# Retention, then two mixtures of experts, on one core: logits two tile steps behind the rows, and the first expert's low weight parts made on VectorE

## The chip, the cores and the metric

One core of one Trainium2 chip runs the whole program in one launch. The metric is the time of one execution in microseconds (us); lower is better. Instructions are issued in order on each of five engines: TensorE (PE, matrix products), VectorE (DVE), ScalarE (ACT), GpSimd (POOL) and SyncE (SP, which here issues most of the transfers).

## The reference

Three layers, each fed by the one before. Only what is computed is kept here.

```python
# 1: batch 8, heads 8, seq 576, head_dim 64
scores = scale * q @ k.T
Dmat   = where(rel >= 0, gamma[h] ** rel, 0.0)       # decay by distance, causal
x      = (scores * Dmat) @ v                         # then laid out as 4608 rows of 512
# 2: 8 experts, each w1 512x1024 and w2 1024x512
logits = x @ w_gate                                  # the row's best expert, by argmax
out    = gate_w * (relu(x @ w1[e]) @ w2[e])
# 3: the same shapes; rows are assigned to experts greedily by their logits,
#    with a capacity of 576 rows for each expert
```

## The kernel before

The 4608 rows are 36 tiles of 128 (lines 141 to 153). Nine tiles make a pair of batches: tiles 0 and 1 of the nine begin the two sequences, and tile 8 holds the last 64 rows of both (`tail`). `attention` (line 128) walks over steps s; in a step each stage function of the table at line 318 is called for tile s - offset, in the order of the table. Every instruction issued there is pinned to that order on its engine (`Pinned`, `InOrder`, lines 107 to 125), and the trace gives all of them the line L114. So a wait on one instruction holds up all that stands behind it on the same engine.

The stages, with the offset of the kernel before:

- `load` (-6): SP loads k, q and v of a tile. `pre` (-2): POOL scales v into `vf`. `kturn`, `qturn` (-2): PE transposes k and q, ACT copies them to `kT` and `qT`.
- `begun` (0): PE multiplies q with the running state, `pO<-qT,st` (nothing for the first tile of a sequence). `scores` (0): PE makes `pS<-qT,kT` and the update of the state (`tp<-vf,k`, not for a tail); DVE masks the scores into `s` in two halves and adds up the state `st`.
- `outputs` (0): PE makes `pO<-s,vf`, eight products with the first half of `s` and eight with the second; DVE scales the result into the tile's rows, `xT`.
- `split` (1): ACT rounds `xT` to a 16-bit high part `xTh`; POOL subtracts, giving the low part `xTl`. Two buffers each.
- `logits` (1): PE multiplies the four blocks of `xTh` and the four of `xTl` with the gate's weights `wg1s`; ACT copies the result into `lgs`.
- `rows` (1): PE transposes `xT`, ACT copies it as `xr`. Three or four tiles make a group, fewer at the end; for a group, `best` (1), `first` (2) and `gates` (3) choose the experts on DVE and ACT, and `store` sends the rows to `Xs` in memory one step after `gates`.

On PE a step thus runs: `begun`, `scores`, the transposes of k, the logits, the output products, the transposes of the rows, the transposes of q.

Two generators run beside the steps, one `next` at the end of a step (lines 328 to 330). `load_half` (line 372) loads the first weights of expert 0 in four pieces (`stage`), from step 4 on, and in steps 13, 16, 19 and 22 it casts a piece to 16 bits on ACT (`w1h`) and makes the low part `w1l` of it. Its argument `dve` says how many pieces' low parts DVE makes; the others take two POOL instructions, a product in place (`stage<-stage`) and a difference. `early` (line 685), from step 30 on, builds lists of rows for expert 0 out of the first 27 tiles, gathers three blocks of 128 rows with POOL's transfers, and two, three and four steps later normalises one block each: a square sum and a scaled copy on ACT, a handful of small operations and a difference on DVE, then a transposing transfer into `xT` of expert 0.

After attention comes `moe1`: expert 0's first products (`ph<-xT,w1h`, line 532) begin with those three blocks. Everything from there on is placed by lists of steps and a scheduler that the change does not touch.

Of the kernel before, what the change touches and what calls it, by code (L numbers as in the profile page):

```python
# [10 lines left out]
F16 = mybir.dt.float16  # L11
# [6 lines left out]
NT = 36  # L18
# [5 lines left out]
SA = 3  # L24
LEAD_IN = 6
CAST = (4, 3)
EARLY = (30, 1)
T0 = (76, 88)
LATE = 3
SOON = 3  # L30
# [97 lines left out]
def attention(k, q, kk_, v, wg1, consts, X, after):  # L128
# [6 lines left out]
    wk = ctx.enter_context(tc.tile_pool(name="wk", bufs=3))  # L135
# [4 lines left out]
    NT = 36  # L140
# [104 lines left out]
        nc.vector.tensor_tensor(pairs(d.xT), d.o, pairs(G[:, d.j]), op=OP.mult)  # L245

    def split(d):
        d.xh = wk.tile([128, 4, 128], F16, name="xTh", bufs=2)
        d.xl = wk.tile([128, 4, 128], F16, name="xTl", bufs=2)
        nc.scalar.activation(d.xh, d.xT, AF.Copy)  # L250
        nc.gpsimd.tensor_tensor(d.xl, d.xT, d.xh, op=OP.subtract)

# [60 lines left out]
    def store():  # L313
        while pend:
            p = pend.pop(0)
            nc.sync.dma_start(Xv[:, p.t0:p.t0 + p.n, :], p.xrows[:, :p.n, :])

    stages = [(load, -LEAD_IN), (split, 1), (pre, -2), (begun, 0), (scores, 0), (kturn, -2), (logits, 1), (outputs, 0), (rows, 1),
              (qturn, -2), (gates, 3), (first, 2), (best, 1)]
    for s in range(-LEAD_IN, NT + 4):  # L320
        store()
        if s == 2 - LEAD_IN:
            nc.sync.dma_start(G[:, 0], consts[:, NC:NC + 512].rearrange("p (h q) -> p h q", q=128))
            k.wg1 = split_gate(k, wg1, "wg1", True)
        for f, off in stages:
            if 0 <= s - off < NT:
                f(D[s - off])
        for g, at0, step in after:
            if s >= at0 and (s - at0) % step == 0:
                next(g, None)  # L330
# [41 lines left out]
def load_half(k, o, w, n, dve=0, spare=False, steps=True, behind=False, spread=False):  # L372


    tc, nc = k.tc, k.nc
    if n == 1:
        o.wp = k.wp2 if k.wn % 2 else k.wp
        k.wn += 1
        o.w1h = o.wp.tile([128, 4, 1024], F16, name="w1h")
        o.w1l = o.wp.tile([128, 4, 1024], F16, name="w1l")  # L380
        h, l, shape, v = o.w1h, o.w1l, [128, 4, 256], w.rearrange("(c p) f -> p c f", p=128)
        at = lambda x, i: x[:, :, i * 256:(i + 1) * 256]
    else:
        if spare:
            o.w2h, o.w2l = (k.wp2.tile([128, 4, 1024], F16, name=x).rearrange("p c (a f) -> p (c a) f", a=2) for x in ("w1h", "w1l"))
        else:
            o.w2h = o.wp.tile([128, 8, 512], F16, name="w2h")
            o.w2l = o.wp.tile([128, 8, 512], F16, name="w2l")
        h, l, shape, v = o.w2h, o.w2l, [128, 2, 512], w.rearrange("(c p) f -> p c f", p=128)
        at = lambda x, i: x[:, 2 * i:2 * i + 2, :]  # L390

    def load(i):
        t = k.wp.tile(shape, F32, name="stage", bufs=3)
        d = nc.sync.dma_start(t, at(v, i))
        if behind:
            tc.keep_in_program_order(d)
        stages.append(t)

    stages = []
    for i in range(3):  # L400
        load(i)
        if spread and i < 2:
            yield
    for i in range(4):
        yield
        t = stages[i]
        if i >= dve:
            if steps:
                pe(k, nc.scalar.activation(at(h, i), t, AF.Copy, scale=128.0))
            else:  # L410
                nc.scalar.activation(at(h, i), t, AF.Copy, scale=128.0)
            pe(k, nc.gpsimd.tensor_scalar(t, t, 128.0, 1.0, op0=OP.mult, op1=OP.mult))
            nc.gpsimd.tensor_tensor(at(l, i), t, at(h, i), op=OP.subtract)
        else:
            d = nc.scalar.activation(at(h, i), t, AF.Copy, scale=128.0)  # L415
            if steps:
                pe(k, d)
            d = nc.vector.scalar_tensor_tensor(at(l, i), t, 128.0, at(h, i), op0=OP.mult, op1=OP.subtract)  # L418
            if steps:
                pe(k, d)  # L420
        if i == (1 if spread else 0):
            load(3)
    if n == 2:
        o.whole = True
# [260 lines left out]
def early(k, X):  # L685


    nc = k.nc
    k.nA = k.cp.tile([128, 4], F32, name="nA")
    OA = k.OH[:, 0, 0:TA]  # L690
    inc = k.lp.tile([128, TA], F16, name="incA", bufs=1)
    nc.vector.tensor_tensor_scan(inc, k.one_h[:, 0:TA], OA, 0.0, op0=OP.mult, op1=OP.add)
    pb = k.tp([128, 2])
    nc.tensor.matmul(pb[:, 0:1], k.lt_h, inc[:, TA - 1:TA], start=True, stop=True)
    nc.tensor.matmul(pb[:, 1:2], k.one_h, inc[:, TA - 1:TA], start=True, stop=True)
    nc.vector.tensor_copy(k.nA[:, 0:2], pb)
    nc.vector.tensor_tensor(k.nA[:, 2:3], k.nA[:, 0:1], inc[:, TA - 1:TA], op=OP.add)
    nc.vector.tensor_scalar(k.nA[:, 3:4], k.nA[:, 0:1], -1.0, 128.0 * SA, op0=OP.mult, op1=OP.add)
    V = k.lp.tile([128, 1, TA + 4], F16, name="VA", bufs=1)
    tables(k, V, TA, inc[:, None, :], k.nA[:, 0:1])  # L700
    nc.vector.scalar_tensor_tensor(OA, inc, k.nA[:, 3:4], OA, op0=OP.is_gt, op1=OP.mult)
    ix, _ = lists(k, V[:, 0, :], TA, k.nA[:, 0:1], k.nA[:, 2:3], SA, k.slot)

    g = k.wp.tile([128, 8, 512], F16, name="w2h").rearrange("p f d -> p (f d)").bitcast(F32)
    h = k.wp.tile([128, 8, 512], F16, name="w2l").rearrange("p f d -> p (f d)")
    sc = k.cp.tile([128, SA, 6], F32, name="scA")
    rows = [gather(k, X[0:128 * TA, :], ix[:, s:s + 1], xg=g[:, W * s:W * (s + 1)]) for s in range(SA)]
    k.early = new_xT(k), []
    yield
    for s in range(SA):  # L710
        yield
        x, c = normalise(k, rows[s], to=(h[:, 1024 * s:1024 * (s + 1)], sc[:, s, :]))
        turn(k, x, k.early[0], s)
        k.early[1].append(c)
# [910 lines left out]
def program(tc, q, kk, v, wg1, w11, w12, wg2, w21, w22, consts, out, dbg=None):  # L1625
    nc = tc.nc
    ctx = ExitStack()
    k = K()
    k.pin = False
    setup(k, tc, nc, ctx, consts)  # L1630
    moe_setup(k, ctx)
    X = tc.dram_tile([128 * NT, W], F32, name="Xs")
    X1 = tc.dram_tile([128 * NS, W], F32, name="X1s")
    LG = tc.dram_tile([128 * NS, 8], F32, name="LGsd")
    k.wgl = split_gate(k, wg2, "wg2")
    select_setup(k)
    k.w = {0: K()}
    attention(k, q, kk, v, wg1, consts, X, [(load_half(k, k.w[0], w11[0], 1, spread=True), *CAST), (early(k, X), *EARLY)])
    open_ffn(k)
    rest = moe1(k, X, X1, w11, w12)  # L1640
    k.pin = False
    overflow(k, X, X1, LG, w11, w12)
    k.wn, k.xn, k.yn = 8, 9, 0
    k.pin = True
    moe2(k, X1, w21, w22, out, rest)
    k.pin = False
    anew(k, X1, w21, w22, out)
    if dbg:
        dbg(k, X, X1, LG)
    k.fctx.close()  # L1650
    ctx.close()
# [25 lines left out]
```

## Time and profile before

| | |
|---|---|
| time, median of 3 runs | 1142.6 us (1140.8 to 1146.78) |
| the profiled execution | 1146.84 us, of which the span from first to last instruction is 1145.0 |
| mean granted TensorE clock in it | 0.965 of full speed |
| PE busy | 1056.3 us, 92% |
| DVE, ACT, POOL busy | 608.1, 436.7, 309.5 us |
| 0 to 200 us: PE busy in each 50 us | 40.91, 46.00, 40.82, 43.67 |
| 200 to 250 us | 40.13, at a mean clock of 0.80 |
| 300 to 400 us: PE busy in each 50 us | 50.00, 50.00 |

Times inside the profile count from the span's start. A line of the timeline gives the start, the duration, the engine, the line and the operation, what is written <- what is read, the shape and how many instructions are merged into it; in brackets how long the engine sat idle before it and what ended that. A granted clock of 1.00 is 2.4 GHz, of 0.50 is 1.2 GHz.

### The profile page before, as it was taken

The page shows a single profiled execution, that of the slowest core. Times are in us where ns is not written, and L with a number is a line of the kernel's source. Part 1 is how long each engine was busy: PE and PEld are TensorE (multiplying, and loading weights), DVE is VectorE, ACT ScalarE, POOL GpSimd, SP SyncE. Part 2 cuts the span into 40 slices and gives each one's busy share as a digit, 9 for nine tenths or more (in the row PEclk, how much of TensorE's full clock was granted, in tenths as well). Part 3 has the DMA queues.
Part 4 walks back from the last instruction along what each step waited for, and adds up shares of the span by engine and source line. Part 5 has one row for each costly group of instructions (what it writes and reads, how often), then busy time and mean ns, then how long its engine had stood idle before and what let it go on. Part 6 is the DMA issues. An engine that isn't in the chain of part 4 may idle for free. (4 is left out here: it accounts for less than half of the span.)

```text
span 1145.0 us, 23324 instructions
## 1 busy us (share of the span) xinstructions
PE 1056.3 (92%) x9159; PEld 686.5 (60%) x9159; DVE 608.1 (53%) x1633; ACT 436.7 (38%) x819; POOL 309.5 (27%) x542
## 2 busy tenths in 40 slices
PE   6997888889999999999979889998889999899996
PEld 5886777645656474756557434655465756567572
DVE  3553445577666564747553366857555656534140
ACT  3453443446455454645441123322222332234240
POOL 5435444223202120212130022323223141531101
PEclk9998999879999999999989899999999999999999
DMA  9999887349667677768884034467375663764221
GB/s 194 214 239 235 195 175 169 59 134 272 172 163 195 170 180 176 185 161 210 217 163 83 11 109 129 129 168 172 109 157 120 158 180 99 203 187 143 83 70 44
DMA packets 307302, 178.43 MB, mean 156 GB/s; under 512 B 241072, under 2 KB 273840, under 8 KB 307184
## 3 DMA queue, kind: packets, MB, share of 16 engines
q1 hardware_dynamic: 296720, 144.51, 53.8%
q0 software_dynamic: 10464, 32.34, 9.2%
q8 instruction: 75, 1.23, 0.5%
q14 instruction: 43, 0.35, 0.1%
HBM read 117.09 MB, written 31.28 MB: 130 GB/s over the span
## 5 line engine op out<-in xcount | busy, mean ns | idle before, releaser
L532 PE MATMUL ph<-xT,w1h 128*128 128x320 f16 (+4 forms) x2048 | 368.1, 296 | 6.0 <-DVE hl L538 3.4
L532 PEld LDWEIGHTS <-w1h 128*128 128x128 f16 x2048 | 197.8, 99 | 81.2 <-issue 16.2
L532 PE MATMUL ph<-xT,w1l 128*128 128x320 f16 (+4 forms) x1024 | 231.2, 296 | 0.0
L558 PE MATMUL py<-w2h,hh 128*128 128x512 f16 x536 | 204.0, 381 | 5.5 <-issue 5.5
L558 PE MATMUL py<-w2l,hh 128*128 128x512 f16 x536 | 204.0, 381 | 0.0
L558 PE MATMUL py<-w2h,hl 128*128 128x512 f16 x536 | 204.0, 381 | 0.0
L558 PEld LDWEIGHTS <-hh 128*128 128x128 f16 x1072 | 103.3, 98 | 122.6 <-issue 7.5
L537 ACT ACTIVATE hh<-ph 128x576 f16<-128x576 f32 (+4 forms) x136 | 83.6, 614 | 192.7 <-PE ph L532 188.0
L538 DVE SCALAR_TENSOR_TENSOR hl<-ph,hh 128x576 f16<-128x576 f32 (+4 forms) x136 | 97.2, 715 | 77.3 <-ACT hh L537 75.9
L532 PEld LDWEIGHTS <-w1l 128*128 128x128 f16 x1024 | 100.0, 99 | 32.8 <-issue 0.8
L418 DVE SCALAR_TENSOR_TENSOR w1l<-stage,w1h 128x1024 f16<-128x1024 f32 x60 | 72.9, 1221 | 59.4 <-ACT w1h L415 58.6
L558 PEld LDWEIGHTS <-hl 128*128 128x128 f16 x536 | 52.5, 98 | 60.3 <-issue 0.8
L418 DVE SCALAR_TENSOR_TENSOR w2l<-stage,w2h 128x1024 f16<-128x1024 f32 x64 | 78.2, 1223 | 10.4 <-ACT w2h L415 8.9
L463 ACT ACTIVATE x1r<-py 128x512 bf16<-128x512 f32 x40 | 23.8, 596 | 120.8 <-PE py L558 81.8
L114 DVE TENSOR_TENSOR s<-pS,ct 128x512 f32<-128x512 f32 x72 | 46.3, 684 | 43.8 <-PE pS L114 43.8
L415 ACT ACTIVATE w2h<-stage 128x1024 f16<-128x1024 f32 x64 | 66.9, 1047 | 5.2 <-DMA stage<-in_moe_w_dram 5.1
L415 ACT ACTIVATE w1h<-stage 128x1024 f16<-128x1024 f32 x60 | 62.3, 1047 | 4.6 <-DMA stage<-in_moe_w_dram 4.6
L114 POOL TENSOR_TENSOR xTl<-xT,xTh 128x512 f16<-128x512 f32 x36 | 41.8, 1161 | 71.0 <-ACT xTh L114 71.0
L449 POOL DMA_INDIRECT xg<-X1s,ix x40 | 46.1, 1152 | 50.6 <-DVE zf L1410 30.9
L1484 POOL DMA_INDIRECT out_dram<-x1r,ti x20 | 23.1, 1154 | 126.8 <-ACT x1r L1483 109.5
L114 DVE TENSOR_TENSOR xT<-pO,G 128x512 f32<-128x512 f32 x36 | 24.9, 692 | 53.3 <-PE pO L114 53.3
L616 POOL COPY x1r<-sc 128x1 f32<-128x1 f32 x37 | 9.8, 265 | 158.6 <-DMA X1s<-x1r 86.8
(354 smaller groups left out, 1456.6 us busy)
## 6 DMA issues: line engine op xcount, KB each, us to landing
stage<-in_moe_w_dram SPq DMA_DIRECT2D x128, 512.0 KB, 4.3
X1s<-x1r SPq DMA_DIRECT2D x33, 257.0 KB, 3.5
k<-in_k_dram SPq DMA_DIRECT2D x32, 256.0 KB, 5.0
q<-in_q_dram SPq DMA_DIRECT2D x32, 256.0 KB, 5.1
v<-in_v_dram SPq DMA_DIRECT2D x32, 256.0 KB, 5.2
Xs<-xr SPq DMA_DIRECT2D x6, 1028.0 KB, 6.4
Xs<-xr SPq DMA_DIRECT2D x3, 771.0 KB, 4.9
k<-in_k_dram SPq DMA_DIRECT2D x8, 128.0 KB, 5.7
```

Source lines behind the costliest of these rows:

```text
L114: return lambda *args, **kw: self.tc.keep_in_program_order(f(*args, **kw))
L415: d = nc.scalar.activation(at(h, i), t, AF.Copy, scale=128.0)
L418: d = nc.vector.scalar_tensor_tensor(at(l, i), t, 128.0, at(h, i), op0=OP.mult, op1=OP.subtract)
L449: nc.gpsimd.indirect_dma_start(out=xg[:M], out_offset=None, in_=src, in_offset=bass.IndirectOffsetOnAxis(ap=gidx[:M], axis=0))
L463: d = nc.scalar.activation(q.bitcast(mybir.dt.bfloat16), x, AF.Square, accum_out=sc[:, 0:1])
L532: pe(k, nc.tensor.matmul(ph[:, z, :b], x[:, c, F], xT[:, y + c, a:a + b], start=i == 0, stop=i == 11))
L537: nc.scalar.activation(oh, src, AF.Relu)
L538: nc.vector.scalar_tensor_tensor(ol, src, 0.0, oh, op0=OP.max, op1=OP.subtract)
L558: pe(k, nc.tensor.matmul(py, x[:, f, S], y[:, f, :], start=i == 0, stop=i == 23))
L616: nc.gpsimd.tensor_copy(xr[:, 513:514], sc[:, 5:6])
L1484: nc.gpsimd.indirect_dma_start(out=out2 if tail else out, out_offset=bass.IndirectOffsetOnAxis(ap=ti, axis=0), in_=y, in_offset=None)
```

## The change

The logits of a tile come two steps after its rows instead of one, and everything that follows them (`best`, `first`, `gates`, the store, the early lists) one step later too; `xTh` and `xTl` get a third buffer, and the loop one more step. `dve` becomes 4 for expert 0's first weights, so that all four low parts are made by one DVE instruction each.

```diff
-EARLY = (30, 1)
+EARLY = (31, 1)
...
     def split(d):
-        d.xh = wk.tile([128, 4, 128], F16, name="xTh", bufs=2)
-        d.xl = wk.tile([128, 4, 128], F16, name="xTl", bufs=2)
+        d.xh = wk.tile([128, 4, 128], F16, name="xTh", bufs=3)
+        d.xl = wk.tile([128, 4, 128], F16, name="xTl", bufs=3)
...
-    stages = [(load, -LEAD_IN), (split, 1), (pre, -2), (begun, 0), (scores, 0), (kturn, -2), (logits, 1), (outputs, 0), (rows, 1),
-              (qturn, -2), (gates, 3), (first, 2), (best, 1)]
-    for s in range(-LEAD_IN, NT + 4):
+    stages = [(load, -LEAD_IN), (split, 1), (pre, -2), (begun, 0), (scores, 0), (kturn, -2), (logits, 2), (outputs, 0), (rows, 1),
+              (qturn, -2), (gates, 4), (first, 3), (best, 2)]
+    for s in range(-LEAD_IN, NT + 5):
...
-    attention(k, q, kk, v, wg1, consts, X, [(load_half(k, k.w[0], w11[0], 1, spread=True), *CAST), (early(k, X), *EARLY)])
+    attention(k, q, kk, v, wg1, consts, X, [(load_half(k, k.w[0], w11[0], 1, 4, steps=False, spread=True), *CAST), (early(k, X), *EARLY)])
```

How instructions move is shown at three places; `-` stands for the kernel before and `+` for the change.

POOL, at the end of step 13, the first piece of expert 0's weights (`xTl` of one tile and `vf` of another above it, those of the next step below):

```order
 L114 TENSOR_TENSOR xTl<-xT,xTh 128x512
 L114 TENSOR_TENSOR vf<-v,ct 128x512
-L114 TENSOR_SCALAR stage<-stage 128x1024
-L114 TENSOR_TENSOR w1l<-stage,w1h 128x4x256
 L114 TENSOR_TENSOR xTl<-xT,xTh 128x512
 L114 TENSOR_TENSOR vf<-v,ct 128x512
```

The two instructions of the piece are gone from POOL, here and at the three other pieces, and the next `xTl` follows `vf` directly.

DVE, at the same place (the group's maximum `mx` and comparison `ge` above, the masked scores, the state and the rows of the next step below):

```order
 L114 TENSOR_REDUCE mx<-lg 128x4
 L114 TENSOR_TENSOR ge<-lg,mx 128x32
+L114 SCALAR_TENSOR_TENSOR w1l<-stage,w1h 128x4x256
 L114 TENSOR_TENSOR s<-pS,ct 128x512 x2
 L114 TENSOR_TENSOR st<-tp,st 128x256
 L114 TENSOR_TENSOR xT<-pO,G 128x2x2x128
```

One instruction comes in, ahead of the next step's two halves of `s`.

ACT, in the first steps of attention (the first copy of logits, `lgs`, is the last row but one):

```order
 L114 ACTIVATE xTh<-xT 128x512
 L114 ACTIVATE kT<-tp 128x512
+L114 ACTIVATE xr<-tp 128x2x128
+L114 ACTIVATE xr<-tp 128x2x64 x2
+L114 ACTIVATE qT<-tp 128x512
+L114 ACTIVATE xTh<-xT 128x512
+L114 ACTIVATE kT<-tp 128x512
 L114 ACTIVATE lgs<-tp 128x16
 L114 ACTIVATE xr<-tp 128x2x128
```

A whole step, with the next tile's `xTh` in it, now stands ahead of the first `lgs`; PE's logits move in the same way. In the last steps of attention the third block's normalising stands in step 35 instead of 34.

## Rows read from the trace of the kernel before

**Rows 1.** The page, its 40 slices of the span: granted clock, in tenths.

```profile
PEclk9998999879999999999989899999999999999999
```

**Rows 2.** Waits from 0 to 245 us: total us, times, longest.

```profile
PE tp L114 <- POOL xTl L114: 23.1, 17, 3.7
...
PE tp L114 <- DMA k<-in_k_dram: 8.1, 3, 5.9
```

**Rows 3.** PE's timeline: output products of a step, and one wait of the logits.

```profile
20.84 1.09 PE L114 MATMUL pO<-s,vf 128*64 128x128 f32 x16
...
56.64 1.09 PE L114 MATMUL pO<-s,vf 128*64 128x128 f32 x16
...
61.37 0.26 PE L114 MATMUL tp<-wg1s,xTl 128*128 128x8 f16 x4 [0.24 <-POOL xTl L114]
61.55 1.09 PE L114 MATMUL pO<-s,vf 128*64 128x128 f32 x16
...
76.87 1.09 PE L114 MATMUL pO<-s,vf 128*64 128x128 f32 x16
...
81.99 1.09 PE L114 MATMUL pO<-s,vf 128*64 128x128 f32 x16
...
97.22 1.09 PE L114 MATMUL pO<-s,vf 128*64 128x128 f32 x16
...
189.26 1.09 PE L114 MATMUL pO<-s,vf 128*64 128x128 f32 x16
...
207.05 1.09 PE L114 MATMUL pO<-s,vf 128*64 128x128 f32 x16
...
228.24 1.87 PE L114 MATMUL pO<-s,vf 128*64 128x128 f32 x16 [0.36 <-DVE s L114]
```

**Rows 4.** Timeline of all engines, 84 to 91 us: a weight piece.

```profile
84.78 1.08 ACT L114 ACTIVATE w1h<-stage 128x1024 f16<-128x1024 f32 x1
...
85.85 1.29 DVE L114 TENSOR_TENSOR s<-pS,ct 128x512 f32<-128x512 f32 x2 [1.29 <-PE pS L114]
...
87.08 2.12 POOL L114 TENSOR_TENSOR w1l<-stage,w1h 128x1024 f16<-128x1024 f32 x1
...
90.36 0.26 PE L114 MATMUL tp<-wg1s,xTl 128*128 128x8 f16 x4 [3.28 <-POOL xTl L114]
```

**Rows 5.** Two stretches: busy us (instructions) of PE, PEld, DVE, ACT, POOL; granted clock.

```profile
91.86:95.27 3.41, 3.41 (x32) 2.75 (x32) 1.13 (x4) 1.96 (x6) 0.51 (x2) 0.50 1.15 218
...
201.08:204.50 3.42, 3.42 (x32) 2.52 (x28) 1.24 (x5) 1.59 (x5) 0.04 (x1) 0.50 0.02 8
```

**Rows 6.** PE's timeline, step 31: the logits after the early gathers.

```profile
200.18 0.26 PE L114 MATMUL tp<-wg1s,xTl 128*128 128x8 f16 x4 [1.94 <-POOL xTl L114]
```

**Rows 7.** Durations: line 418 on the page; `xTl`, min/median/max ns.

```profile
L418 DVE SCALAR_TENSOR_TENSOR w1l<-stage,w1h 128x1024 f16<-128x1024 f32 x60 | 72.9, 1221 | 59.4 <-ACT w1h L415 58.6
...
L114 POOL TENSOR_TENSOR xTl<-xT,xTh x36: 1149/1159/1202, 19.4 to 232.8; 128x512 f16<-128x512 f32 x36
```

**Rows 8.** Timeline of DVE, step 33: `s` behind the normalising.

```profile
212.65 1.28 DVE L114 TENSOR_TENSOR s<-pS,ct 128x512 f32<-128x512 f32 x2
```

**Rows 9.** Timeline, 222 to 237 us; and expert 0's `xT`: transpose to landing.

```profile
223.25 0.72 ACT L114 ACTIVATE xr<-tp 128x256 f32<-128x256 f32 x3 [1.43 <-PE tp L114]
...
226.59 1.23 SPq L114 DMA_TRANSPOSE xT<-w2l  x1
...
236.09 0.80 PE L532 MATMUL ph<-xT,w1h 128*128 128x384 f16 x2 [0.81 <-ACT xr L114]
...
DMA to landing us min/median/max: 3.2/3.4/3.7
```

**Rows 10.** Tile 16's k: issue, first reading; the page's median to landing.

```profile
70.65 1.10 SPq L114 DMA_DIRECT2D k<-in_k_dram  x1
...
86.35 0.65 PE L114 MATMUL tp<-ct,k 128*128 128x128 f32 x4
...
k<-in_k_dram SPq DMA_DIRECT2D x32, 256.0 KB, 5.0
```

## The prediction, made before the change was run

> **What bounds the kernel now.** I read the page first: TensorE (PE) is the busiest engine throughout, and its granted clock falls below full speed mostly in the first fifth of the span and again in short dips later [rows 1]. The change touches only attention (up to about 236 us) and what starts expert 0, so I asked for the list of waits of that stretch: PE stands idle 23.1 us, 17 times, until GpSimd (POOL) has made the low half of a tile's rows (`xTl`), against 8.1 us for loads of k, all of which lie in the first 16 us [rows 2]. Then I read PE's timeline for the start of the output products (`pO<-s,vf`), which come once per tile step, because their distance is the length of a step with everything in it [rows 3]. An undisturbed step takes 81.99 - 76.87 = 5.12 us. Three tiles in nine have less to multiply (the first two of a pair have no state, the last updates none): 61.55 - 56.64 = 4.91 us, of which 0.24 us is a wait for `xTl`, so about 4.68 us. From tile 1's products (20.84) to tile 35's (228.24) are 34 steps, 24 long and 10 short: 24 x 5.12 + 10 x 4.68 = 169.7 us if nothing disturbed them. They take 207.4 us. So 37.7 us are lost, and the question is which part the change gives back. PE bounds the undisturbed step: within it nothing on PE waits.
>
> **Where the 37.7 us lie.**
> - Four steps carry a piece of expert 0's first weights. ScalarE (ACT) casts it, POOL then scales and subtracts, and the next `xTl` stands behind that on POOL: POOL is through with `w1l` at 89.2, and PE, which was ready at 87.1, waits 3.28 us [rows 4]. The step after it runs at the lower of the clock's two levels (1.2 instead of 2.4 GHz): PE is busy all of 91.86 to 95.27 at a granted 0.50 [rows 5]. The two steps take 97.22 - 81.99 = 15.23 us instead of 10.24 [rows 3], 4.99 us more: 3.28 of them the wait, so about 1.7 the slow clock. There are four such places: 20.0 us.
> - The early lists and their row gathers (line 702 on) fall into step 30. From 189.26 to 207.05 two steps take 17.79 us instead of 10.24 [rows 3], 7.55 us more. 1.94 us of that is again a wait for `xTl` [rows 6], which in the order of the code stands behind three gathers on POOL, and about 1.7 us the slow clock that followed it (201.08 to 204.50 at 0.50 [rows 5]).
> - The last three steps, in which three early row blocks are normalised, take 228.24 - 207.05 = 21.19 us instead of 14.92 [rows 3]: 6.27 us.
> - What is left, 37.7 - 20.0 - 7.55 - 6.27 = 3.9 us, is short waits for `xTl` like the 0.24 us in rows 3.
>
> **The change, part by part.**
> Logits two steps behind, with a third buffer for `xTh` and `xTl`: no instruction is added; PE's eight small products per tile and ACT's copy `lgs` move one step down. `xTl` then has a whole step, some 5 us, of slack. Even the 3.28 us delay stays inside that, so every wait of PE for `xTl` should go. What is late next at these places? After 90.36 PE goes on to the output products, whose `s` was ready at 87.14 [rows 4]: nothing.
> Low parts on VectorE (DVE): four pairs of POOL instructions go (the second of a pair takes 2.12 us [rows 4]), four DVE instructions of 1.22 us come [rows 7]. They stand ahead of the next step's `s` in DVE's order. In the step of rows 4, ACT's cast ends at 85.86, so `w1l` would run from 85.95 to 87.17, and the halves of `s` (1.29 us for both) would be ready at 87.82 and 88.46 instead of 86.5 and 87.14. PE gets to the output products at 81.99 + 5.12 = 87.11: it waits 0.7 us for the first half and 0.1 to 0.2 for the second. I take 0.9 us each, 3.6 us for four. Bounds: 0.6 us (the first half alone, a little earlier) and 1.3 us (all of `w1l`). The lower clock does not follow in my sum; if it did, 1.7 us each.
> So the four places give 20.0 - 3.6 = 16.4 us, and the short waits 3.9 us.
> The early lists move one step down with their work. Their own chain stays on PE's path with the slow clock it brings; the 1.94 us and the slow clock behind it go: 3.6 us (1.9 if the clock stays slow anyway).
> The normalising moves to the ends of steps 33, 34 and 35. There the wait for `xTh` and `xTl` goes, but `s` was held up too, by the DVE part of the normalising: in step 33 it starts at 212.65, its first half is ready at 213.29, and PE would be there at 207.05 + 5.12 = 212.17 [rows 3, 8]. So a wait of 1.3 us remains in step 34 and, since one more DVE instruction (line 868) now stands ahead of `s` there, I put 1.8 us in step 35: 3.1 us for the 6.27, a gain of 3.1 us; less 1.7 us for each time the clock falls there.
> The price of the move stands at the end. The third block is now normalised in the last step, and expert 0's first product needs its transposed rows. Before, from the copy `xr` of that step (223.25) to the transpose's issue went 3.34 us, and it lands 3.4 us after [rows 9]: 6.75 us. `xr` starts when the output products (1.09 us at full clock, 1.87 at the lower one [rows 3]) and the row transposes behind them are done, 1.7 to 2.9 us after their start by my estimate, so the rows are there 8.5 to 9.7 us after tile 35's products. Expert 0 now starts 236.09 - 228.24 = 7.85 us after them. I take 1.2 us lost (0.6 to 1.9). The chain of the last logits (split, logits, best, gates, store) has the same parts as before, and nothing of moe1 or moe2 is moved.
> SyncE's queue issues every store of X one step later and the second weights' first pieces a little earlier; loads run ahead. k of tile 16 is issued at 70.65, needs some 5.0 us, and is first read at 86.35 [rows 10]: 10.7 us of cover, built up while PE ran undisturbed steps from a start where it waited for loads. A steady 5 us step does not use it up.
>
> Sum: 16.4 + 3.9 + 3.6 + 3.1 - 1.2 = **25.8 us**. The profiled execution took 1146.8 us (span 1145.0): 1121.0. It lies 4.2 us above the median of 1142.6, so against the median I forecast **1117 us**.
>
> A rule that speaks against the change: the Trainium skill, GPSIMD Engine Reference, Specifications, says that GpSimd shares its SBUF interfaces with VectorE and that DVE instructions with two SBUF inputs contend with it. `w1l` is one, and would run beside `xTl`. The trace shows little of it: `xTl` takes 1149 to 1202 ns over all 36 [rows 7], among them those beside DVE work, the normalising subtraction included. The rule is a rival below.
>
> **The rivals.**
> 1. Pauses of 1 to 2 us are enough for the lower clock. For: the 1.94 us wait at 200.18 was followed by it [rows 5, 6]. Against: the 0.24 us ones were not [rows 1, 3]; pauses of 0.9 lie between. Price: 1.7 us at each of the four `w1l` and in steps 34 and 35: 10.2 us. Gain 15.6, 1127 us. Chance 0.20.
> 2. `w1l` and `xTl`, which touch SBUF at the same time, run one after the other, so that `s` comes up to 1.16 us later in four steps: 4.6 us, gain 21.2, 1121.4 us. For: both read two tiles there. Against: the spread in rows 7. Chance 0.08. By the skill's rule above this is what would be seen.
> 3. The loads become the bound once the steps are short. Against: rows 10. If the cover were gone by tile 16 and each later step took 5.6 us, 20 steps x 0.6 = 12 us: 1129 us. Chance 0.04.
> 4. The waits stay under another name, because at those places something else is as late (`s`, the state): then 1142 us, no change. Rows 4 speak against it. Chance 0.06.
> 5. Slower: the pauses at `s` keep the clock at its lower level through the rest of attention. Each of the 22 steps from 14 to 35 then costs 1.7 us more, 37.4 us: 37.4 - 25.8 = 11.6 us slower, 1154 us. It decides from 16 slow steps on (25.8 / 1.7 = 15.2). Against: at full load to 80 us the clock stayed full [rows 1]. Chance 0.04.
>
> **How the numbers follow.** My forecast holds with 0.58. The bounds in the sum: at best 0.6 us for each `w1l` and for the end, and the first wait before tile 1's products: 29 us, 1113.5; with runs that differ by 6 us before, 1109. At worst rivals 1 and 2 take it to 1127, with a us of spread 1128. The range 1109 to 1128 leaves out rivals 3 to 5 and little else. Half a per cent (5.7 us) is about what a measurement can tell from no change. Faster by more: 0.58 + 0.20 + 0.08 + 0.04 = 0.90. Same: 0.06. Slower: 0.04.
>
> **What would show it.** In the profile after: no wait of PE for `xTl` between 24 us and step 35; four `w1l` on DVE of about 1.22 us, each followed by some 0.9 us of PE waiting for `s`; no lower clock between 90 and 190 us; tile 35's products at about 20.84 + 169.7 + 3.6 + 4.0 + 3.1 = 201 us; expert 0's first product some 9 us behind them; the stretch from there to the end as long as before. Wrong would be: slow clock after each `w1l` (rival 1), `w1l` or `xTl` well over 1.2 us (rival 2), waits of PE for k, q or v after 30 us (rival 3), or an expert 0 that starts more than 10 us after tile 35's products.

## The result, and the profile after

| | before | after | after, run again |
|---|---|---|---|
| time, median (range) in us | 1141.7 (1137.2 to 1146.8), 4 runs | 1111.4 (1106.8 to 1112.8), 4 runs | 1114.5 (1112.9 to 1121.5), 5 runs |
| ratio to before, 95% interval | | 0.9726 (0.9676 to 0.9776) | 0.9765 (0.9741 to 0.9790) |
| the profiled execution | 1146.84 | 1111.32 | 1112.94 |
| tile 1's products to tile 35's | 207.4 | 179.0 | 182.0 |
| from there to expert 0's first product | 7.85 | 9.18 | 9.49 |
| from there to the end of the span | 909.0 | 900.9 | 897.9 |

The last column is the same kernel, run again beside the experiments (its before: 1143.3). The change made the kernel faster by 2.3 to 2.7%; 1117 had been forecast, in a range of 1109 to 1128. Between the medians lie 30.3 us. Between the spans of the two profiled executions lie 35.6 us, since the profiled one of the kernel before was the slowest of its four: 0.5 ahead of tile 1's products, 28.4 between tile 1's and tile 35's products (forecast: 27.0), 1.3 lost behind them (1.2), and 8.1 in the stretch to the end, where the forecast had none.

The list of waits of the kernel after, 0 to 245 us, answers to [rows 2]: PE's 23.1 us for `xTl` are 1.0, and that one is the very last tile's. What stands there now is `s`.

```profile
PE tp L114 <- DMA k<-in_k_dram: 8.4, 3, 6.3
PE pO L114 <- DVE s L114: 6.7, 6, 2.0
...
PE tp L114 <- ACT xTh L114: 2.0, 1, 2.0
...
PE tp L114 <- POOL xTl L114: 1.0, 1, 1.0
```

PE's timeline answers to [rows 3]: the output products around the first weight piece, those of tiles 34 and 35, the last logits, and expert 0's first product.

```profile
75.12 1.09 PE L114 MATMUL pO<-s,vf 128*64 128x128 f32 x16
80.24 1.09 PE L114 MATMUL pO<-s,vf 128*64 128x128 f32 x16
86.02 1.26 PE L114 MATMUL pO<-s,vf 128*64 128x128 f32 x16 [0.59 <-DVE s L114]
91.30 1.09 PE L114 MATMUL pO<-s,vf 128*64 128x128 f32 x16
96.42 1.09 PE L114 MATMUL pO<-s,vf 128*64 128x128 f32 x16
...
192.03 1.26 PE L114 MATMUL pO<-s,vf 128*64 128x128 f32 x16 [1.62 <-DVE s L114]
...
199.35 1.68 PE L114 MATMUL pO<-s,vf 128*64 128x128 f32 x16 [1.97 <-DVE s L114]
...
205.20 0.26 PE L114 MATMUL tp<-wg1s,xTh 128*128 128x16 f16 x4 [1.98 <-ACT xTh L114]
...
208.53 0.82 PE L532 MATMUL ph<-xT,w1h 128*128 128x384 f16 x2 [1.79 <-DMA xT<-w2l]
```

The two steps with the piece take 91.30 - 80.24 = 11.06 us where 15.23 had been [rows 3] and 10.24 is undisturbed. A table by stretch (columns as in [rows 5], and last the share and GB/s of the DMA engines) shows the clock: full behind the 0.59 us pause, half behind the 1.62 and 1.97 us ones.

```profile
86.02:91.30 5.28, 5.28 (x84) 4.36 (x85) 3.42 (x10) 1.73 (x6) 2.96 (x4) 1.00 1.20 228
193.20:196.60 3.40, 3.40 (x50) 2.93 (x50) 1.60 (x7) 1.76 (x6) 0.00 (x0) 0.50 0.91 281
200.00:203.40 3.40, 3.22 (x26) 2.43 (x24) 1.24 (x5) 1.29 (x5) 0.22 (x2) 0.51 0.06 11
```

The timelines of VectorE and GpSimd at that piece answer to [rows 4], and `xTl`'s durations (min/median/max ns) to [rows 7]. The low part takes 1.23 us and `s` follows at once; but the `xTl` beside it takes 1.68 us, and so do four of 36. None did before [rows 7].

```profile
84.14 1.23 DVE L114 SCALAR_TENSOR_TENSOR w1l<-stage,w1h 128x1024 f16<-128x1024 f32 x1 [1.45 <-ACT w1h L114]
85.28 1.28 DVE L114 TENSOR_TENSOR s<-pS,ct 128x512 f32<-128x512 f32 x2
...
84.70 1.68 POOL L114 TENSOR_TENSOR xTl<-xT,xTh 128x512 f16<-128x512 f32 x1 [3.91 <-ACT xTh L114]
```

```profile
L114 POOL TENSOR_TENSOR xTl<-xT,xTh x36: 1155/1159/1682, 20.2 to 205.2; 128x512 f16<-128x512 f32 x36
```

### The profile page after: what moved, and what is told of

Read it like the earlier page. It is cut to its first block, busy times and chain, and to the rows that moved or that the text cites. A ratio compares the mean times of both kernels' runs of the same rounds, so it can differ in the third digit from the quotient of the medians.

```text
span 1109.4 us, 23387 instructions
## 1 busy us (share of the span) xinstructions
PE 1044.6 (94%) x9159; PEld 677.4 (61%) x9159; DVE 611.5 (55%) x1637; ACT 434.4 (39%) x819; POOL 301.1 (27%) x534
## 3 DMA queue, kind: packets, MB, share of 16 engines
q8 instruction: 75, 1.23, 0.5%
## 5 line engine op out<-in xcount | busy, mean ns | idle before, releaser
L463 ACT ACTIVATE x1r<-py 128x512 bf16<-128x512 f32 x40 | 23.8, 596 | 117.7 <-PE py L558 75.4
L1484 POOL DMA_INDIRECT out_dram<-w2T,ti x20 | 21.9, 1093 | 118.4 <-ACT w2T L1483 97.1
```

Of the source, the lines that this page charges most:

```text
L463: d = nc.scalar.activation(q.bitcast(mybir.dt.bfloat16), x, AF.Square, accum_out=sc[:, 0:1])
L1484: nc.gpsimd.indirect_dma_start(out=out2 if tail else out, out_offset=bass.IndirectOffsetOnAxis(ap=ti, axis=0), in_=y, in_offset=None)
```

## The experiments

Distances below are read from each run's profiled execution, times are medians. All are ratios to the kernel before on the same chip.

| run | tile 1's to tile 35's products | to expert 0's first product | from there to the end | time | ratio (95%) |
|---|---|---|---|---|---|
| logits alone | 182.1 | 9.0 | 902.7 | 1113.4 | 0.9739 (0.9707 to 0.9772) |
| VectorE alone | 193.0 | 8.0 | 907.4 | 1130.0 | 0.9875 (0.9856 to 0.9895) |
| low part behind | 179.9 | 8.3 | 899.4 | 1112.8 | 0.9731 (0.9717 to 0.9745) |
| low part twice | 193.7 | 8.3 | 900.0 | 1127.4 | 0.9880 (0.9858 to 0.9902) |
| normalising in mid-step | 182.5 | 5.6 | 900.8 | 1110.6 | 0.9735 (0.9710 to 0.9760) |
| store by GpSimd | 180.9 | 9.1 | 899.4 | 1113.1 | 0.9756 (0.9736 to 0.9776) |
| before, more code | 207.4 | 6.5 | 901.3 | 1136.4 | 0.9946 (0.9925 to 0.9967) |
| three things | 178.2 | 7.4 | 902.7 | 1105.3 | 0.9682 (0.9657 to 0.9707) |
| three, low part on GpSimd | 184.4 | 7.8 | 900.8 | 1106.3 | 0.9693 (0.9666 to 0.9720) |
| three, gathers later | 175.7 | 7.9 | 902.0 | 1107.0 | 0.9684 (0.9661 to 0.9707) |
| gathers later, alone | 181.6 | 9.3 | 901.8 | 1114.4 | 0.9762 (0.9744 to 0.9780) |

### Each half of the change alone

Logits alone, against the kernel after:

```diff
-load_half(k, k.w[0], w11[0], 1, 4, steps=False, spread=True)
+load_half(k, k.w[0], w11[0], 1, spread=True)
```

> The changed kernel with the low parts of expert 0's first weights back on GpSimd; the logits stay two steps behind. Theory (the loss was PE waiting for xTl, and the shift of the logits alone removes it): GpSimd's 3.2 us fit into the step of slack that xTl now has, so no wait of PE for xTl comes back, and the four waits of PE for s (0.6 to 1.3 us in the changed kernel's steps with a w1l) go: four pairs of steps at 10.24 us instead of 11.06, tile 35's products at 196 us instead of 199.35, a time near 1108 us against 1111.4 of the changed kernel. Rival (the move to VectorE carries the gain): the delay on GpSimd turns up as a wait for vf or xTl, 3 to 5 us at each of the four places, tile 35's products at 211 to 219 us and a time of 1123 to 1131.

The steps 13 to 25 came out as the theory has them: every pair of steps with a piece takes its undisturbed time (10.24 us, and 9.31 at the second piece, whose tiles are short ones), PE waits there neither for `xTl` nor for `s`. Up to tile 31 the run gained 3.34 us on the kernel after. It lost them again in step 33, by a wait that neither theory names: PE waited 5.09 us for an `xTl`, which stood on GpSimd behind the early gathers. So tile 35's products came at 201.58 us, not at 196, and the time missed its 1108. Timeline of this run:

```profile
171.44 0.18 PE L114 MATMUL tp<-incA,lt_h 128*128 128x1 f16 x1 [0.49 <-DVE incA L114]
...
175.13 0.56 SPq L114 DMA_DIRECT2D Xs<-xr  x1
...
181.58 1.21 POOL L114 DMA_INDIRECT w2h<-Xs,ix  x1 [11.84 <-DVE s L114]
...
186.54 0.27 PE L114 MATMUL tp<-wg1s,xTl 128*128 128x8 f16 x4 [5.09 <-POOL xTl L114]
```

The lists are ready some 3 us after their first product (171.44), but the gathers read the rows of tiles 24 to 26, whose store SyncE issued only at 175.13, behind its loads; it took 6.45 us more until the first gather. (The releaser named in that row had long been done.) The same rows before, where the store was 3.9 us ahead of the lists' first product, and after, where it was 1.5 us ahead:

```profile
188.03 0.56 SPq L114 DMA_DIRECT2D Xs<-xr  x1
191.88 0.18 PE L114 MATMUL tp<-incA,lt_h 128*128 128x1 f16 x1 [0.50 <-DVE incA L114]
195.23 1.21 POOL L114 DMA_INDIRECT w2h<-Xs,ix  x1 [5.20 <-DVE ix L114]
```

```profile
174.23 0.56 SPq L114 DMA_DIRECT2D Xs<-xr  x1
175.68 0.18 PE L114 MATMUL tp<-incA,lt_h 128*128 128x1 f16 x1 [0.50 <-DVE incA L114]
179.90 1.20 POOL L114 DMA_INDIRECT w2h<-Xs,ix  x1 [5.92 <-DMA Xs<-xr]
```

VectorE alone, against the kernel before:

```diff
-load_half(k, k.w[0], w11[0], 1, spread=True)
+load_half(k, k.w[0], w11[0], 1, 4, steps=False, spread=True)
```

> The kernel before with only the four low parts moved to VectorE; the logits stay one step behind. Theory (two separate ways to the same 20 us): the four waits of 3.28 us for xTl and the slow clock behind them go, and about 0.8 us of waiting for s or for a late xTl comes at each place, so 4 x (4.99 - 0.8) = 16.8 us; the short waits for xTl, the 7.55 us of the early lists and the 6.27 us of the last three steps stay: tile 35's products at about 211.4 us, a time near 1125. Rival (without the shift VectorE's 1.2 us come on top of the step's chain from s over xT to xTl): 2 to 3 us lost at each place with the slow clock behind it, tile 35's products at 217 to 222, a time of 1130 to 1136.

Between the two, with tile 35's products at 215.07 us and a time at the rival's edge: the first place takes 6.38 + 5.28 = 11.66 us, 1.4 more than undisturbed, since here PE stands waiting for just the `xTl` that w1l slows to 1.68 us. Rows of PE and GpSimd, first place:

```profile
89.42 0.25 PE L114 MATMUL tp<-wg1s,xTl 128*128 128x8 f16 x4 [1.11 <-POOL xTl L114]
...
87.69 1.68 POOL L114 TENSOR_TENSOR xTl<-xT,xTh 128x512 f16<-128x512 f32 x1 [3.90 <-ACT xTh L114]
```

So the two halves are two ways to the same 20 us. The shift alone reaches the ratio of the whole change (0.974 against 0.973 and 0.977); the low parts on VectorE alone reach less than half of it, and on top of the shift they give nothing that can be measured.

### The low part: behind its cast, and twice

```diff
-        yield
+        if i == 0 or not spread: yield
...
-            if steps:
-                pe(k, d)
+            if steps: pe(k, d)
+            if spread: yield
             d = nc.vector.scalar_tensor_tensor(at(l, i), t, 128.0, at(h, i), op0=OP.mult, op1=OP.subtract)
```

> The changed kernel with each low part on VectorE one call later, that is three steps behind its cast, where its input is long there. Theory (s is late because w1l waits for ScalarE's cast, while VectorE stands idle for 1.3 us ahead of s): w1l runs in that idle time, the four waits of PE for s (0.6 to 1.3 us) shrink below 0.2 us, tile 35's products come at 196 to 197 us instead of 199.35, a time near 1108.5. Rival (VectorE's own 1.2 us is what holds s up): the waits stay at 0.6 us and more, only in steps 16, 19, 22 and 25, and the time stays at 1111.

The waits went, all but one of 0.25 us: up to tile 31 the run is 3.25 us ahead of the kernel after, and no `xTl` takes over 1.20 us. The time did not follow: steps 32 and 33 took 9.04 and 8.21 us, again with a wait for `xTl` behind the gathers (2.93 us) and half the clock behind the lists. The cause of the pauses at `s` is settled, their worth of 3 us not visible in the time.

```diff
-            d = nc.vector.scalar_tensor_tensor(at(l, i), t, ...
+            for _ in range(1 + spread): d = nc.vector.scalar_tensor_tensor(at(l, i), t, ...
```

> The changed kernel with each of the four low parts of expert 0's first weights made twice in a row on VectorE, 1.22 us more each. Theory (PE's pauses at these places grow from 0.6 to 1.3 us to about 1.8 to 2.5, and pauses of that size are followed by a stretch at half clock, as the 1.6 and 2.0 us ones of the last steps were): 4 x (1.2 + about 1.5) = 11 us more up to tile 35's products and three or four new stretches at half clock between 85 and 140 us; a time near 1124. Rival (in full steps a single pause of 2 us does not lower the clock; it fell in the last steps because PE had less to do there): 4 x 1.2 = 5 us more, no half clock before 175 us, a time near 1118.

Each place lost 2.1 us more in waiting, not 1.2. Durations in ns (min/median/max); the wait of the first piece; then the stretch behind it and the one behind the second piece's wait of 3.27 us:

```profile
L114 DVE SCALAR_TENSOR_TENSOR w1l<-stage,w1h x8: 1224/1641/2061, 84.0 to 143.0; 128x1024 f16<-128x1024 f32 x8
L114 POOL TENSOR_TENSOR vf<-v,ct x36: 1034/1045/2021, 8.4 to 198.2; 128x512 f32<-128x512 f32 x36
```

```profile
87.93 1.26 PE L114 MATMUL pO<-s,vf 128*64 128x128 f32 x16 [2.69 <-DVE s L114]
```

```profile
87.93:93.20 5.27, 5.27 (x84) 4.37 (x84) 3.41 (x10) 1.72 (x5) 1.83 (x3) 1.00 1.20 231
106.80:110.20 3.40, 3.40 (x22) 2.73 (x22) 1.17 (x4) 0.99 (x4) 0.00 (x0) 0.50 1.15 236
```

The second low part meets GpSimd's `xTl` and `vf`, and both sides pay: 2.06 us for 1.22, 2.02 for 1.04. Behind waits of 2.69 us the clock stayed full twice; with those of 3.27 and 2.80 us it fell, for 3.4 and 6.8 us (from 106.78, behind the wait, and from 123.85, 1.1 us before the wait's end). Neither theory holds as put: a pause that long lowers the clock sometimes.

### The early lists and the normalising

```diff
+    normal = lambda d: next(after[1][0], None) if d.t >= EARLY[0] + 2 else None
-    stages = [..., (scores, 0), (kturn, -2), ...
+    stages = [..., (scores, 0), (normal, 0), (kturn, -2), ...
-            if s >= at0 and (s - at0) % step == 0:
+            if s >= at0 and (s - at0) % step == 0 and (at0 < 30 or s < at0 + 2):
```

> The changed kernel with the three early blocks normalised in the middle of steps 33, 34 and 35, behind the masked scores s, instead of at the ends of these steps, ahead of the next s. Theory (s waits for the normalising, because VectorE runs in order and the normalising waits for ScalarE): PE's waits for s of 1.6 and 2.0 to 2.4 us in steps 34 and 35 go, with the half clock behind them, about 5 us; and since ScalarE has the last xTh ahead of nothing and the third block's transposed rows are there earlier, expert 0's first product comes 5 to 6 us after tile 35's products instead of 9.2, about 3.5 us: 8 us in all, a time near 1104. Rival (the rows of tile 33 to 35 now wait behind the normalising on VectorE, and the gathered rows are not there so early): the waits come back at the row transposes or at the gathered rows, 1.5 us or more per step, and the time stays within 3 us of the changed kernel's 1111 to 1114.

Expert 0's first product came 5.6 us after tile 35's, as the theory has it. Its other half failed: PE waited 2.79 us for the `xTl` behind the gathers, ScalarE waited 3.14 us for the gathered rows in step 33, VectorE's difference `w2l` took 2.94 us instead of 0.75 while GpSimd worked off `vf`, `xTl`, `vf`, and PE's next products waited 1.1 and 1.6 us for the output products' buffer, which VectorE empties.

```diff
-        pend.append(p)
+        nc.gpsimd.dma_start(Xv[:, p.t0:p.t0 + p.n, :], p.xrows[:, :p.n, :]) if p.t0 == 24 else pend.append(p)
```

> The changed kernel with one store moved: the rows of tiles 24 to 26, which the early gathers read, are stored from GpSimd's queue right behind their gates instead of from SyncE's queue behind the loads of tile 35. Theory (the gathers start 5.7 to 6.5 us after that store is issued, and SyncE issues it 1.5 us before to 2.7 us after the early lists' first product, from execution to execution; GpSimd waits that long with the next xTl behind it): the store goes out about 3 us earlier, the gathers start when the lists are ready, some 3 us after the lists' first product instead of 4.2 to 10; step 32 takes at most 7.5 us, step 33 5.1; tile 35's products come 178 to 179 us after tile 1's in every execution (before: 179.0 and 182.0), a time of 1109 to 1111. Rival (the gathers wait for something else, their own descriptors or the memory): they start as late as before, the distance stays at 179 to 182 us and the time at 1111 to 1114.

The gathers started 180.43 - 177.09 = 3.3 us after the lists' first product and PE's wait for `xTl` was gone, as the theory has it. Yet step 32 took 9.43 us, since the clock fell behind the lists (half of full, 179.2 to 182.6). PE's two pauses in the lists' chain (0.5 to 0.9 and 1.1 us) are in both profiles of the kernel after too: the clock stayed full behind them in the first and fell in the second (179.6 to 183.0). So the place costs 2.4 or about 4 us by chance, and the time shows no gain.

```diff
+    yield
     rows = [gather(k, X[0:128 * TA, :], ix[:, s:s + 1], xg=g[:, W * s:W * (s + 1)]) for s in range(SA)]
     k.early = new_xT(k), []
-    yield
```

> The changed kernel with the early gathers alone one step later (at the end of step 32). Theory (the gathers' wait for the store of tiles 24 to 26 is what makes step 32 and 33 of the changed kernel vary): GpSimd waits under 1 us for that store, no wait of PE for xTl in steps 32 to 34; tile 35's products come 179 to 181 us after tile 1's (179.0 with the clock staying up behind the lists, 1.7 more where it falls), a time of 1109 to 1112 with a smaller spread than the 9 us of the second look at the changed kernel. Rival (gathers later are rows later): the first normalising waits for its rows at the end of step 33 and s with it, the distance grows to 182 us or more, the time to 1113 to 1117.

A miss: PE waited for no `xTl` in those steps and the spread was 3.2 us, but the store was issued still later (178.13) and the gathers waited as long, while the lists' chain met an `xTl`: a small VectorE operation of it took 1.23 us instead of 0.3.

### The stretch that the change does not touch

> The changed kernel once more. From expert 0's first product to the end it took 900.9 us and the kernel before 909.0, where nothing was changed. Theory (that stretch varies from execution to execution, by waits of the last layer's choice of experts for weights and by the slow clock behind them): it comes out anywhere from 900 to 909 us here, and in the other three runs too, whether they carry the logits' shift or not. Rival (the change itself shortens it by 8 us): 900 to 902 here and in the two runs with the shifted logits, 908 to 910 in the run without. Time 1107 to 1113 by both.

The shifted kernels lie at 898 to 903 us, before and VectorE alone, with logits one step behind, at 909.0 and 907.4: nearer the rival. (The time, 1114.5, lies above the range that both gave.) Compared product by product, most of the difference stands at one place, a jump between the second layer and the third: every engine branches past the loop of line 996, which serves experts with too many rows and of whose body no row stands in the trace. PE's row there in before and in the first profile of the kernel after:

```profile
647.78 0.61 PE L558 MATMUL py<-w2h,hh 128*128 128x512 f16 x1 [5.50 <-issue]
```

```profile
615.27 0.39 PE L558 MATMUL py<-w2h,hh 128*128 128x512 f16 x1 [2.17 <-DVE key L1306]
```

PE's order there is the same; but the page counts 23324 instructions before, 23323 with VectorE alone, and 23387 after. PE's own stream has 31 more after: the same products and weight loads, and 31 more waits issued as instructions. To test whether the place of the code is what counts, the kernel before got 16 products more, far away:

```diff
-    def across(x):
+    def across(x, n=1):
...
-        for c in range(4):
+        for c in range(4) if n == 1 else [0, 1, 2, 3] * n:
...
-        pt = across(x.rearrange("p h d -> p (h d)"))
+        pt = across(x.rearrange("p h d -> p (h d)"), 3 if d.t < 2 and name == "kT" else 1)
```

> The kernel before, with the transposes of k of tiles 0 and 1 issued three times each, 16 products more in the first 15 us, where PE waits for loads; the values are the same. It tests the 8 us that the change won behind attention. Theory (the logits' shift made PE's instruction stream some 31 instructions longer, so that at the jump into the loop of the last expert of the second layer its next piece of code is there 3.3 us sooner; the gap of PE at that jump was 5.5 and 5.1 us in the two kernels with logits one step behind, 2.2 to 2.4 us in the four with logits two steps behind): 32 instructions more do the same here, the gap is 2.2 to 2.4 us, the half clock behind it 3.4 us long instead of 6.8, and the time 4 to 5 us below the kernel before, some 1138. Rival (the gap hangs on the order or the data of what is computed, not on where the code lies): the gap stays 5.1 to 5.5 us and the time is that of the kernel before or up to 1 us above it.

PE's row at the jump, and the stretch behind it, in this run; then the stretch in before:

```profile
642.24 0.39 PE L558 MATMUL py<-w2h,hh 128*128 128x512 f16 x1 [2.19 <-DVE key L1306]
```

```profile
643.30:646.70 3.40, 3.40 (x14) 1.42 (x13) 1.42 (x3) 0.28 (x1) 1.02 (x1) 0.50 0.00 0
646.70:650.00 3.30, 3.30 (x18) 1.30 (x17) 1.25 (x5) 0.11 (x1) 0.58 (x1) 0.99 0.21 80
```

```profile
644.80:651.60 6.80, 3.82 (x10) 1.35 (x11) 1.10 (x4) 0.69 (x1) 1.26 (x3) 0.50 0.12 41
```

The gap fell from 5.50 to 2.19 us, the half clock from 6.8 to 3.4 us, and the time by 5.6 us (0.5%): more work, and faster. In this run and in the ten kernels with shifted logits, whose PE streams are 31 to 33 instructions longer than before's, the gap is 2.2 to 2.4 us.

The traces show what fills the gap. The transfers of code have queues of their own, of the kind `instruction`; here is what queue q8 started in PE's gap (packets, MB, share), in before (642.28 to 647.78) and then after (613.10 to 615.27):

```profile
q8 instruction: 2, 0.03, 3.1%
```

```profile
q8 instruction: 1, 0.02, 2.8%
```

In before both pieces of code, some 16 KB each, start inside the gap, at 643.44 and 646.87, and PE goes on at 647.78. After, the first of the two starts at 611.12, 2.0 us ahead of the gap, and only the second, at 614.43, lies in it. VectorE alone has two in its gap (5.06 us); this run and the others with a gap of 2.2 to 2.4 us have one, and the piece before it starts 1.5 to 3.2 us ahead of the gap. That 31 to 33 instructions more let PE ask for the first piece earlier is the reading that fits; the order itself is not in the trace.

### A version that beats both

The store by GpSimd, the low part behind its cast (both with the edits above), and the normalising in three parts, half a step apart. `go(s, part)` does one part of block s: 0 is the square sum, 1 the scale and the scaled copy, 2 the difference and the transfer. The lines that order the parts:

```diff
...
+    for todo in ((), (), ((0, 0),), ((0, 1), (1, 0)), ((0, 2),), ((1, 1), (2, 0)), ((1, 2), (2, 1)), ((2, 2),)):
+        for s, part in todo: go(s, part)
+        yield
```

> The changed kernel with three things together: each low part w1l on VectorE one call behind its cast; the store of tiles 24 to 26 on GpSimd's queue; and the normalising of the three early blocks cut into three parts (square sum; scale and scaled copy; difference and transposing transfer) that stand half a step apart, so that no part on VectorE waits for one on ScalarE. Theory (what is left to win between the first and the last tile is three waits: for s behind w1l, 3.3 us; for xTl behind the early gathers and the half clock behind them, 0 to 8 us from execution to execution; for s behind the normalising, with its half clock, 5 us; and expert 0's first product waits for the last logits, 6 us behind tile 35's products, instead of the third block, 9.2): 171 to 173 us from tile 1's products to tile 35's (the changed kernel: 179.0 and 182.0), 177 to 179 to expert 0's first product (188.2 and 191.5), no w1l beside an xTl and so every xTl at 1.2 us; a time of 1099 to 1103. Rival (mixing them only moves the waits, as in the run that moved the normalising whole): 177 us or more to tile 35's products, a time of 1106 to 1111.

At 1105.3 us it beats the kernel before by 3.2%, and the kernel after by some 9 us where that was run again, clear of the intervals, and by 6 in the first result, where the intervals overlap. It misses the theory by two to six. The timeline of steps 32 and 33, and a table of two stretches, show why:

```profile
177.33 1.10 POOL L114 DMA_INDIRECT w2h<-Xs,ix  x1 [5.35 <-DMA Xs<-xr]
...
180.89 4.38 DVE L114 TENSOR_TENSOR ge<-ge,w 128x24 f32<-128x24 f32 x1
180.95 1.16 POOL L114 TENSOR_TENSOR xTl<-xT,xTh 128x512 f16<-128x512 f32 x1
182.07 1.04 POOL L114 TENSOR_TENSOR vf<-v,ct 128x512 f32<-128x512 f32 x1
...
183.07 1.15 POOL L114 TENSOR_TENSOR xTl<-xT,xTh 128x512 f16<-128x512 f32 x1
184.19 1.03 POOL L114 TENSOR_TENSOR vf<-v,ct 128x512 f32<-128x512 f32 x1
...
186.44 1.26 PE L114 MATMUL pO<-s,vf 128*64 128x128 f32 x16 [2.19 <-DVE s L114]
```

```profile
181.00:185.20 4.20, 3.25 (x62) 2.68 (x60) 4.20 (x1) 2.78 (x9) 4.20 (x5) 1.00 0.60 154
188.10:191.50 3.40, 3.40 (x34) 2.74 (x34) 1.28 (x7) 1.99 (x6) 0.19 (x1) 0.50 0.02 5
```

GpSimd had issued the store 3.9 us ahead of the lists' first product (168.76 and 172.64), and its gathers still waited 5.35 us for it. Then an operation of VectorE that takes 0.17 us elsewhere stood for 4.38 us, as long as GpSimd worked off two steps' work without a break; `s` came 2.19 us late, and the clock fell. The two last runs follow from it. One puts the low part back on GpSimd (the edit of the first experiment, without that of the low part behind its cast):

> The run before it in this list with the low parts w1l back on GpSimd, as in the kernel before. Theory (with the logits two steps behind, GpSimd's 3.2 us at each of the four places are covered, so it makes no difference where w1l is made as long as PE waits for neither): the same steps 13 to 25, 171 to 173 us from tile 1's products to tile 35's, a time within 3 us of that run. Rival (GpSimd's longer queue comes back as a wait, or the loads of k, q and v, whose lead shrinks by some 0.4 us a step here, run out): waits of PE for k, q or xTl between 85 and 170 us, a time over 3 us longer.

The time is the same within the intervals, and the pairs of steps with a piece take their undisturbed time. The distance, 184.4 us, is not the theory's, and the profiled execution shows the rival's wait: PE stood 4.40 us for a tile's k, which SyncE had issued at 147.42, behind a load of weights and a store, and which landed some 9 us later (the page's median: 5.5). So where w1l is made makes no difference once the logits are shifted, but the loads are near their limit.

The other moves the gathers one step down:

```diff
+    yield
     rows = [gather(k, X[0:128 * TA, :], ix[:, s:s + 1], xg=g[:, W * s:W * (s + 1)]) for s in range(SA)]
...
-    for todo in ((), (), ((0, 0),), ((0, 1), (1, 0)), ((0, 2),), ((1, 1), (2, 0)), ((1, 2), (2, 1)), ((2, 2),)):
+    for todo in ((), (), ((0, 0), (1, 0)), ((0, 1), (2, 0)), ((0, 2), (1, 1)), ((1, 2), (2, 1)), ((2, 2),)):
```

> The run with all three things, with the early gathers one step later (at the end of step 32; the lists stay in step 31), and the parts of the normalising half a step later at the start. Theory (in that run GpSimd stood 5.4 us in the gathers' wait for the store, then worked off two steps' xTl and vf in a row from 180.95 to 185.2, and in just that time a VectorE instruction of 0.2 us, ge, took 4.38 us, which made s 2.2 us late with the half clock behind it: VectorE's operations on two SBUF operands stand still while GpSimd works without a break): the store has landed when the gathers come, GpSimd never falls behind, no ge over 0.5 us, no wait of PE for s over 0.6 us in steps 32 to 35: 172 to 175 us from tile 1's products to tile 35's instead of 178.2, a time of 1099 to 1103 against 1105.3. Rival (the long ge has another cause, or the gathers take their time from the normalising instead): the distance stays at 177 us and more, the time at 1104 to 1108.

No long `ge` (0.17 us at 182.24), no wait for `s` over 0.9 us, steps 33 to 35 at 5.25, 4.64 and 5.12 us: the mechanism holds. But the lists' chain in step 32 now met GpSimd's work, PE waited 2.08 us in it, the clock was halved for 6.8 us, and step 32 took 11.18 us. The distance fell by 2.6 us, the time did not.

## Why the prediction was right, point by point

- **The bound and the 37.7 us lost.** Right: with the logits shifted, a pair of steps with a piece that is not held up takes the 10.24 us. Only the second piece was misread: its tiles are short, its pair takes 9.31 us undisturbed, and it took 15.33 before. So the four places cost 21.1 us, not 20.0, and the short waits had 1.1 less; the sum stays.
- **Every wait of PE for `xTl` goes.** Right in the profile of the kernel after, and right at the four pieces in every run with the logits shifted. "What is late next" was asked there alone. At the lists I let 1.94 us of waiting go and missed that GpSimd, in its wait for the store of tiles 24 to 26, holds the next `xTl`. Before, SyncE issued that store 3.9 us ahead of the lists' first product; after, 1.5 us ahead, and in that kernel run again 1.3 us behind (178.34 and 177.08). My sentence on the queue looked only at the loads' cover, and a store stands at its end. The slack hides it in both profiles of the kernel after, but not in logits alone (5.09 us), the low part behind (2.93) and normalising in mid-step (2.79).
- **0.9 us for each low part.** Right: the places cost 0.82, 1.15, 0.94 and 0.82 us, 3.7 in all against 3.6 forecast, and no lower clock behind pauses of 0.59 to 1.18 us.
- **3.95 us left at the lists.** Measured 2.4 in one profile, where the clock stayed full behind the lists' chain, and 4.9 in the other, where it fell (3.92 and 0.95 us over 5.12). That the forecast lies between them is in part luck: it has the slow clock of the chain in it, and the clock behind the chain differs from execution to execution.
- **3.1 us left at the normalising.** Under-sized by 0.8: 5.12 + 6.33 + 7.32 = 18.77 us against 14.92. The waits are 1.62 and 1.97 us where I put 1.3 and 1.8, which is 0.5 of it. The clock fell behind both, which the text names and the sum leaves out; the second fall lies behind tile 35's products and so outside these steps.
- **1.2 us lost at the end.** Right: 1.3 and 1.6.
- **"Nothing of moe1 or moe2 is moved", so that stretch stays as long.** This is the step that failed. The order did not move, but the code did: some 5 us of the gain (3.3 at the jump, the rest the clock behind it) come from where PE's code lies, as the kernel before with 16 repeated products shows. The other 3 to 6 us of that stretch are waits that differ from execution to execution, such as one of 3.40 us (line 1325) in the profile of before. By the attention part alone, from tile 1's products to expert 0's first, the forecast of 25.8 us stands between the 27.1 and 23.8 us of the two profiles. That the median came out 5.6 us under the forecast is about what this stretch gave.
- **The rivals.** The first (lower clock behind short pauses) is true of the two pauses of 1.6 and 2.0 us, not of the four at the pieces. The second (chance 0.08) has its mechanism right and its price wrong. The contention is there, and `xTl` well over 1.2 us was one of my signs of being wrong: 1.68 us beside `w1l`, 1.16 alone. I had looked for it in the durations of `xTl` alone, where the normalising's difference overlaps one by just 0.19 us. The same trace has it on VectorE's side: the `ge` of 232.94 us, beside the last `xTl`, takes 1.09 us instead of 0.18. The loss at the pieces falls on GpSimd, where the shift had just made room, and not on `s`. The Trainium skill (GPSIMD Engine Reference, Specifications) says that VectorE instructions with two SBUF inputs contend with GpSimd. The runs agree, by the 1.68 us.

## What to carry to other kernels

When a wait has a delay as its cause, giving the consumer a step of slack and removing the delay are two ways to the same gain: price them apart, for they do not add, and the slack also absorbs delays not yet known. Where steps get shorter, look at what is last in each in-order queue (here one store behind the loads), for it comes relatively later. Before crediting a few tenths of a per cent to an idea, compare the stretches that it does not touch: code that only lies elsewhere gave 0.5% here, and a profile can be of the slowest execution.

## What the runs showed of the hardware that was not expected

- The cost of a taken jump changes with the length of the code ahead of it: PE's gap at one was 5.1 and 5.5 us in two kernels, with two pieces of code moved in the gap, and 2.2 to 2.4 in the eleven whose PE stream is 31 to 33 instructions longer, with one. The Trainium skill (Runtime: NRT & Kernel Launch, Instruction fetch mechanics) says that a taken branch to code outside the part being prefetched must have it fetched first. The traces agree: in all fourteen profiles PE goes on 0.7 to 0.9 us after the last of these pieces started.
- VectorE and GpSimd block each other for longer than one instruction: 0.17 us became 4.38 us beside four GpSimd operations in a row. The Trainium skill (SBUF — State Buffer, SBUF: two separate sides) calls the shared ports "an exclusive lock, not a bandwidth split", held for the whole instruction. The pairs in these runs agree (a low part of 2.06 us for 1.22 and a `vf` of 2.02 for 1.04, where they meet), the 4.38 us go beyond one instruction.
- The same pauses of PE (0.5 to 0.9 and 1.1 us at the lists, 2.7 to 3.3 us with the low part made twice) were followed by half the clock in some places and executions, not in others. What decides was not found.
